# One SBUF arena for all phases, memory rows made token-major inside the chains, and 8-row stationaries

## The chip, the cores and the metric

The kernel runs on one core of one Trainium2 chip. The metric is the device time of one execution in microseconds. Three executions of the kernel before took 4016.91, 4025.89 and 4031.85 us, median 4025.89.

## The reference

A transformer block with a recurrent memory, forward and backward. x is 2048 tokens of 448 values, in bf16. `h = x + A(layernorm(x))`, `h2 = h + B(layernorm(h))`, and the outputs are h2 and the gradients of x, mem0 and the seven weights for a given gradient of h2.

A cuts the tokens into 64 segments of 32. Segment s sees 8 memory tokens in front of its own 32 (40 rows in all); with 16 heads of 256 (4096 columns) it computes

```
h = concat(mem, xs);  q, k, v = h Wq, h Wk, h Wv
p = softmax(mask(q k^T / 16));  o = (p v) Wo
mem = o[:8]            # the next segment's memory
out = o[8:]
```

where the mask hides earlier rows' view of later keys, and memory rows see everything. B is `(silu(x Wg) * (x Wu)) Wd` with 1792 hidden columns. Memory ties the 64 segments into a chain, forward and, for the gradients, back.

## The kernel before

Four phases follow each other in one program; the Tile framework orders each engine's instructions, and what stands under `k.prio.crit()` goes ahead of the rest.

**Start.** SP loads Wq and Wo, POOL loads Wv and Wk (L97 and L98 in `load_rows_padded`, L257). Behind them on SP stand mem0 (L270) and every other tile of x (L280), whose layernorm goes to XN in DRAM.

**forward_chain.** A tile is 128 tokens, four segments; r = 0..3 is a segment's place in it. Per segment PE runs `wpass` for q and k (L378: 128 matmuls each of 40 columns), scores (L406), the 8 memory rows' v (L413), the softmax's transposes (L442), P V (L450), the memory rows' output through Wo (L460) and four small matmuls that turn the 8 rows into the next segment's memory columns (L469, L472). The memory rows of V come through SBUF: `v_sb` is copied into V by DMAs on SP and ACT (L431). As filler PE computes v for a later tile (L359; through `vstg` to Vx in DRAM, read back at L369) and, at r = 3, the tile's output px (L492). L460 takes 32 columns per chunk as stationary (`oTm`, 8 used, 24 zero) and writes strips of 32 rows, one for each j % 4, of a bank from the pool `ps` (6 banks). For the weight gradients the chain leaves in DRAM: Q and K and V per segment, P, the tile's head outputs feature-major (X_o, 1 MB, L499 on SP), and of the 8 memory rows M_o (L481) and MT (L485), each by a POOL copy and a POOL DMA.

**ffn_phase.** Eight groups of two tiles, forward and backward. SP transposes WdT (L112, L114), WgT (L525) and WuT (L526) from DRAM around the first group's loads (L548, L556); its gate, up and hidden values leave token-major by SP transposes into `tstg` and POOL stores (L537, L538). At its end dh goes to DH and, in bf16, to DHb.

**backward_chain.** SP first loads WoT (L112, L114), then WkT, WvT and WqT (L303), all by DMA transposes, then dhx from DHb (L660). Per segment, in reverse: dO = do WoT (L703), its transposed copy dO_sb (L709, a DMA transpose on SP), dP (L715), dS, three head products (L694) and three passes of the memory rows' gradient (L746, again 32-column stationaries, into one bank `pH`) which give the earlier segment's memory gradient (L753, L755). SP loads vT, Q_sb, K_sb by DMA transposes (L681, L683, L685). POOL writes DMT (L765), copies each of k, v, q's memory columns into one buffer `x8` and stores it to M_k, M_v, M_q (L768, L769); at r = 0 px (L774) and the three X stores of 1 MB (L776).

**tail_phase.** Weight gradients: operands in token-major rows are multiplied with other rows, summed over 20 blocks, 16 tiles and 4 blocks of 16 x 8 memory rows. `load_half` brings one half (2048 of 4096 columns) of X_o, X_v, X_k or X_q: 16 DMA transposes on SP (L811), then four times a POOL load of M (L816), two packing copies (L819 DVE, L820 ACT) and a DMA transpose from SBUF (L822), into a ring of 36 buffers. The other operand is DC (from DHb, and DMT) or HC (from XN, and MT), whose memory rows come by POOL loads, copies and PE transposes (L834 to L839). `rows_by_d` (L869) makes dWo and dWdown, `d_by_e` (L853) the others: per block six matmuls of 128 stationary columns and, for the last 64 of 448, two of 64 columns side by side, into seven accumulators. Results go through three buffers `wres` to ACT's DMA queue. In between POOL, DVE and ACT make dx (L902 to L909). Gate, up and down read DGP, DU (L917) and Zt (L934) by plain loads.

## Time and profile before

The profiled execution took 4031.56 us, its span is 4029.7 us.

| engine | busy us | share of the span |
|---|---|---|
| PE | 3318.0 | 82% |
| DVE | 1369.7 | 34% |
| ACT | 809.4 | 20% |
| POOL | 785.7 | 19% |

| stage | from us | to us |
|---|---|---|
| start, until PE's first q pass | 0 | 58.5 |
| forward chain | 58.5 | 1320.3 |
| FFN's loads before its first matmul | 1320.3 | 1357.4 |
| FFN | 1357.4 | 1695.5 |
| until the backward chain's first matmul | 1695.5 | 1775.9 |
| backward chain | 1775.9 | 3066 |
| tail | 3066 | 4029.7 |

A line such as "L853 PE MATMUL acc<-xt,HC" names the source line, the engine, the operation, the tile written and the tiles read; x is a count. SPq is SP's queue, where DMA transposes hold the engine while their descriptors are made. "DMA share" is the busy share of the core's 16 DMA engines; it can read slightly over 1. "PEclk" is the granted clock of PE as a fraction of full speed. In a window's row the first number is its length, then each engine's busy time and count.

### The profile page before, as it was taken

To read this page: it belongs to the slowest core of one execution; us is meant where nothing else is said; L and a number is where in the kernel's file an instruction comes from. 1 tells how busy PE (TensorE), PEld (TensorE's weight loads), DVE (VectorE), ACT (ScalarE), POOL (GpSimd) and SP (SyncE) were. 2 spreads that over 40 slices of the span, in tenths; PEclk is the share of its full clock that TensorE was granted. 3 is DMA by queue.
4 is the path that set the end of the run, shared out by engine and by line. 5 is a ranking of instruction groups with operands and counts; after the bars stand their busy time and mean duration, and the time that the engine had idled before them with its cause. 6 is when DMAs were issued, how large, how long until landed. Compare 5 with 4: busy or idle time off the path is not lost.

```text
span 4029.7 us, 120360 instructions
## 1 busy us (share of the span) xinstructions
PE 3318.0 (82%) x53974; PEld 2056.4 (51%) x53974; DVE 1369.7 (34%) x3032; ACT 809.4 (20%) x1914; POOL 785.7 (19%) x1669
## 2 busy tenths in 40 slices
PE   3888988998988588738898898898996566887999
...
PEclk9999999999998799869899999998997788998999
...
GB/s 236 139 136 147 140 146 140 142 148 142 133 136 115 207 166 192 165 225 158 172 181 154 164 184 149 152 164 167 172 170 161 188 207 171 159 167 159 196 183 48
DMA packets 1201433, 653.00 MB, mean 162 GB/s; under 512 B 1093012, under 2 KB 1127604, under 8 KB 1191316
## 3 DMA queue, kind: packets, MB, share of 16 engines
...
## 4 chain that ended last, share of the span: by engine, by line
PE 62%; DMA 16%; SPq 7%; issue 5%; DVE 4%; ACT 3%; POOL 1%; ACTq 0%; DVEq 0%; POOLq 0%
PE acc L853 11%; PE psf L378 11%; PE psf L746 7%; PE fx L774 6%; PE psf L703 5%; DMA dO_sb<-doT 4%; PE psf L460 4%; SPq L811 3%; PE acc L869 2%; PE psf L694 2%; PE psf L413 2%; PE fx L492 2%; PE fx L359 2%; PE psf L469 1%; DMA out_dram<-wres 1%
## 5 line engine op out<-in xcount | busy, mean ns | idle before, releaser
L853 PE MATMUL acc<-xt,HC 128*128 128x512 bf16 (+1 forms) x1920 | 446.8, 405 | 95.3 <-ACT wres L77 70.4
L853 PEld LDWEIGHTS <-HC 128*128 128x128 bf16 (+1 forms) x1920 | 157.9, 103 | 384.2 <-issue 278.7
L703 PE MATMUL psf<-do_roll,WoT_sb 128*128 128x40 bf16 x8192 | 217.6, 180 | 85.3 <-POOL do_roll L663 80.5
L703 PEld LDWEIGHTS <-WoT_sb 128*128 128x128 bf16 x8192 | 216.4, 96 | 97.2 <-issue 82.8
L869 PE MATMUL acc<-DC,xt 128*128 128x448 bf16 x640 | 147.6, 393 | 114.9 <-ACT wres L77 35.5
L378 PEld LDWEIGHTS <-Wq_sb 128*128 128x128 bf16 x8192 | 231.3, 100 | 19.6 <-issue 8.2
L378 PE MATMUL psf<-hT_roll,Wq_sb 128*128 128x40 bf16 x8192 | 231.6, 184 | 5.7 <-DVE hT_roll L472 5.4
L75 DVE CAST wres<-acc 128x512 bf16<-128x512 f32 (+1 forms) x87 | 56.5, 669 | 496.1 <-PE acc L853 277.1
L378 PE MATMUL psf<-hT_roll,Wk_sb 128*128 128x40 bf16 x8192 | 219.3, 180 | 0.5 <-issue 0.4
L378 PEld LDWEIGHTS <-Wk_sb 128*128 128x128 bf16 x8192 | 213.8, 97 | 0.9 <-issue 0.7
L869 PEld LDWEIGHTS <-xt 128*128 128x128 bf16 x864 | 87.9, 104 | 213.2 <-issue 79.6
L75 DVE CAST doT<-psf 128x480 bf16<-128x480 f32 (+1 forms) x128 | 73.6, 575 | 245.7 <-PE psf L703 245.7
L77 ACT CAST wres<-acc 128x512 bf16<-128x512 f32 (+2 forms) x87 | 47.6, 551 | 539.4 <-PE acc L853 264.3
L359 PE MATMUL fx<-Wv_sb,hx 128*128 128x512 bf16 x512 | 135.4, 386 | 17.2 <-DMA hx<-XN 9.9
L413 PE MATMUL psf<-Wv_sb,memT_pad 128*32 128x512 bf16 x2048 | 147.8, 381 | 0.2
L460 PE MATMUL psf<-Wo_sb,oTm 128*32 128x448 bf16 x2048 | 143.4, 436 | 2.8
L774 PE MATMUL fx<-WqT_sb,blkq 128*128 128x448 bf16 x512 | 130.8, 371 | 0.0
L774 PE MATMUL fx<-WvT_sb,blkv 128*128 128x448 bf16 x512 | 128.2, 369 | 0.0
L746 PE MATMUL psf<-WvT_sb,dvm 128*32 128x448 bf16 x2048 | 123.9, 388 | 3.4 <-DVE dvm L75 0.4
L774 PE MATMUL fx<-WkT_sb,blkk 128*128 128x448 bf16 x512 | 124.6, 354 | 0.0
L492 PE MATMUL fx<-Wo_sb,xblk 128*128 128x448 bf16 x512 | 118.1, 356 | 0.0
L746 PE MATMUL psf<-WqT_sb,dqm 128*32 128x448 bf16 x2048 | 110.7, 357 | 3.5 <-DVE dqm L75 0.4
...
## 6 DMA issues: line engine op xcount, KB each, us to landing
...
KT<-kT_363 SPq DMA_DIRECT2D x32, 512.0 KB
...
VG<-V_365 SPq DMA_DIRECT2D x32, 512.0 KB
...
VG<-V_366 SPq DMA_DIRECT2D x32, 512.0 KB
...
```

The source lines that it names most:

```text
L75: nc.vector.tensor_copy(out=out, in_=in_)
L359: nc.tensor.matmul(pv[:, 0:512], lhsT=hx[t][:, kc, :], rhs=Wv_sb[:, kc, n * 512:(n + 1) * 512], start=(kc == 0), stop=(kc == KC - 1))
L378: nc.tensor.matmul(pss[b][:, jj * L:(jj + 1) * L], lhsT=W_sb[:, kc, c * P:(c + 1) * P], rhs=hT_roll[:, kc, sl, :], start=(kc == 0), stop=( ...
L413: nc.tensor.matmul(pV[b][32 * j:32 * j + 32, 0:512], lhsT=memT_pad[:, kc, :], rhs=Wv_sb[:, kc, n * 512:(n + 1) * 512], start=(kc == 0), st ...
L460: nc.tensor.matmul(pO[32 * (j % 4):32 * (j % 4) + 32, 0:D], lhsT=oTm[:, j, :], rhs=Wo_sb[:, cj(j), :], start=(j < 4), stop=(j >= MC - 4), ...
L492: nc.tensor.matmul(px[:, 0:D], lhsT=xblk[:, j, :], rhs=Wo_sb[:, cj(j), :], start=(j == 0), stop=(j == MC - 1))
L703: nc.tensor.matmul(pss[b][:, jj * L:(jj + 1) * L], lhsT=WoT_sb[:, kc, c * P:(c + 1) * P], rhs=do_roll[:, kc, sl, :], start=(kc == 0), stop ...
L746: nc.tensor.matmul(pH[32 * (j % 4):32 * (j % 4) + 32, 0:D], lhsT=dm_pad[nm][:, j, :], rhs=WT[:, cj(j), :], start=(wi == 0 and j < 4), stop ...
L774: nc.tensor.matmul(px[:, 0:D], lhsT=blk[nm][:, j, :], rhs=WT[:, cj(j), :], start=(wi == 0 and j == 0), stop=(wi == 2 and j == MC - 1))
L811: nc.sync.dma_start_transpose(out=x_t[:].rearrange("p (j n) -> p j n", n=P), in_=dr["X_" + nm][t][:, hf * 2048:(hf + 1) * 2048])
L853: nc.tensor.matmul(o, lhsT=lhs, rhs=rhs_of(b, g), start=(b == 0), stop=(b == nblk - 1), skip_group_check=True)
L869: nc.tensor.matmul(pa[i][:, 0:D], lhsT=lhs_of(b, i), rhs=rhs_of(b), start=(b == 0), stop=(b == nblk - 1))
```

## The change

Two kinds of thing change: where data lives, and how the memory rows reach the tail.

All phases share three SBUF areas, W (124 KB per partition), A (65 KB) and B (8.25 KB), each one tile; every buffer is a fixed range of one, and a phase's buffers lie over those of the phase before, so that an instruction waits for the last readers of its range and not for a pool to close. PSUM is one pool of 5 `ps` banks, 2 `fx` and 1 `po`. In the order rows the areas are called arW, arA and arB; the line numbers tell what is meant.

In the forward chain a finished tile of head outputs is transposed to token-major by two DMA transposes on SP through the two staging buffers of v_proj and stored by POOL (`to_token_major`, L390, L392); the memory rows of 16 segments are gathered in `mblk` and `mh` and go the same way, as blocks 16 to 19 of X_o and XN (L504). In the backward chain the memory rows' do are gathered in `dmr` and become blocks 16 to 19 of DHb (L783). M_k, M_v, M_q are stored straight from the stationaries; M_o, MT, DMT and the copies into `x8` are gone. The tail loads X_o plainly (L843), X_v, X_k and X_q by DMA transposes as before (L845), and the memory blocks of v, k, q by a POOL load, two packing copies and 16 PE transposes with two copies out of PSUM (L859). `d_by_e` runs the full matmuls of four blocks (L875) before their half-width ones (L880). The ring has 33 buffers, results have 8. The memory stationaries of L460 and L746 have 8 columns; the 24 rows of each strip that they no longer write are zeroed once, in a bank of their own. At the start x and mem0 stand first on SP and ACT, and POOL loads all weights in the order Wq, Wk, Wv, Wo.

```diff
+class _Arena:
+
+
+    def __init__(self, pool, name, kb):
+        self.n = int(kb * 512)
+        self.t = pool.tile([P, self.n], BF16, name=name)
...
-            m0f = work.tile([P, DP], BF16, name="m0", tag="xtmp", bufs=2)
-            m0 = m0f[0:M, :]
-            nc.sync.dma_start(out=m0[:, 0:D], in_=MEM0)
...
-            for t in range(NT):
-                x_tf = work.tile([P, DP], BF16, name="x_t0", tag="xtmp", bufs=2)
-                (nc.sync if t % 2 == 0 else nc.gpsimd).dma_start(out=x_tf[:, 0:D], in_=X2[t * P:(t + 1) * P, :])
...
-        k.load_rows_padded(Wv_sb, Wv2, nc.gpsimd)
-        k.load_rows_padded(Wq_sb, Wq2, nc.sync)
-        k.load_rows_padded(Wk_sb, Wk2, nc.gpsimd)
-        nc.sync.dma_start(out=Wo_sb[:], in_=Wo2.rearrange("(c p) d -> p c d", p=P))
...
+    pO = k.po1()
+    nc.vector.memset(pO[:], 0.0)
...
+    nc.sync.dma_start(out=v_sb[0:M, 0:D], in_=MEM0)
...
+    def stats(t):
+        q = nc.sync if t % 2 == 0 else nc.scalar
+        x_t = xblk_b[0].rearrange("p a b -> p (a b)")[:, (t % 4) * DP:(t % 4) * DP + D]
+        q.dma_start(out=x_t, in_=X2[t * P:(t + 1) * P, :])
...
+    for t in range(2):
+        stats(t)
+    pad_rows(k, Wq_sb, k.Wq2, nc.gpsimd)
+    pad_rows(k, Wk_sb, k.Wk2, nc.gpsimd)
+    pad_rows(k, Wv_sb, k.Wv2, nc.gpsimd)
+    nc.gpsimd.dma_start(out=Wo_sb, in_=k.Wo2.rearrange("(c p) d -> p c d", p=P))
...
+    for t in range(2, NT):
+        stats(t)
...
+    def to_token_major(blk, t):
+        for hf in range(2):
+            ot = stg()
+            nc.sync.dma_start_transpose(out=ot.rearrange("p (a b) -> p a b", b=P),
+                                        in_=blk[:, 16 * hf:16 * hf + 16, :].rearrange("p c n -> p (c n)"))
+            nc.gpsimd.dma_start(out=dr["X_o"][t][:, hf * 2048:(hf + 1) * 2048], in_=ot)
...
-                k.evac(oTm[:, 12 * b:12 * b + n, 0:M], v[:, :, SEG:L], "vsv"[b])
-            pO = k.ps1()
+                k.evac(o8[:, 12 * b:12 * b + n, :], v[:, :, SEG:L], "vsv"[b])
             for j in range(MC):
-                nc.tensor.matmul(pO[32 * (j % 4):32 * (j % 4) + 32, 0:D], lhsT=oTm[:, j, :], rhs=Wo_sb[:, cj(j), :],
+                nc.tensor.matmul(pO[32 * (j % 4):32 * (j % 4) + M, 0:D], lhsT=o8[:, j, :], rhs=Wo_sb[:, cj(j), :],
...
-        o8 = work.tile([P, 32, M], BF16, name="o8", bufs=2)
-        nc.gpsimd.tensor_copy(out=o8[:], in_=oTm[:, :, 0:M])
-        nc.gpsimd.dma_start(out=dr["M_o"][s], in_=o8[:].rearrange("p c m -> p (c m)"))
-        m8 = work.tile([P, KC, M], BF16, name="m8", bufs=2)
-        nc.gpsimd.tensor_copy(out=m8[:], in_=hT_roll[:, :, sl, SEG:L])
-        nc.gpsimd.dma_start(out=dr["MT"][s], in_=m8[:].rearrange("p c m -> p (c m)"))
...
+        nc.gpsimd.tensor_copy(out=mh[:, :, jm * M:(jm + 1) * M], in_=hT_roll[:, :, sl, SEG:L])
+        nc.gpsimd.tensor_copy(out=mblk[:, :, jm * M:(jm + 1) * M], in_=o8)
...
-            nc.sync.dma_start(out=dr["X_o"][t], in_=xblk[:].rearrange("p c n -> p (c n)"))
...
+            to_token_major(xblk, t)
+        if jm == 15:
+            to_token_major(mblk, NT + s // 16)
+            mrow = stg()
+            nc.sync.dma_start_transpose(out=mrow[:, 0:DP].rearrange("p (a b) -> p a b", b=P),
+                                        in_=mh.rearrange("p c n -> p (c n)"))
+            r0 = (NT + s // 16) * P
+            nc.gpsimd.dma_start(out=dr["XN"][r0:r0 + P, :], in_=mrow[:, 0:DP])
...
+    transposed_rows(k, WoT_sb, k.Wo2, woT_tmp)
...
+    prep_tile(NT - 1)
+    load_seg(NSEG - 1)
+    for (Wsrc, WT) in ((k.Wk2, WkT_sb), (k.Wv2, WvT_sb), (k.Wq2, WqT_sb)):
+        nc.sync.dma_start_transpose(out=WT, in_=Wsrc)
...
-                    nc.tensor.matmul(pH[32 * (j % 4):32 * (j % 4) + 32, 0:D], lhsT=dm_pad[nm][:, j, :], rhs=WT[:, cj(j), :],
+                    nc.tensor.matmul(pH[32 * (j % 4):32 * (j % 4) + M, 0:D], lhsT=d8[nm][:, j, :], rhs=WT[:, cj(j), :],
...
-        d8 = work.tile([P, KC, M], BF16, name="d8", bufs=2)
-        nc.gpsimd.tensor_copy(out=d8[:], in_=do_roll[:, :, sl, SEG:L])
-        nc.gpsimd.dma_start(out=dr["DMT"][s], in_=d8[:].rearrange("p c m -> p (c m)"))
...
+        nc.gpsimd.tensor_copy(out=dmr[:, :, jm, :], in_=do_roll[:, :, sl, SEG:L])
+        if jm == 0:
+            nc.sync.dma_start_transpose(out=dhx, in_=dmr.rearrange("p c s m -> p (c s m)"))
+            r0 = (NT + s // 16) * P
+            nc.gpsimd.dma_start(out=dr["DHb"][r0:r0 + P, :], in_=dhx.rearrange("p c n -> p (c n)"))
         for nm in "kvq":
-            x8 = work.tile([P, 32, M], BF16, name="x8", bufs=1)
-            nc.gpsimd.tensor_copy(out=x8[:], in_=dm_pad[nm][:, :, 0:M])
-            nc.gpsimd.dma_start(out=dr["M_" + nm][s], in_=x8[:].rearrange("p c m -> p (c m)"))
+            nc.gpsimd.dma_start(out=dr["M_" + nm][s], in_=d8[nm].rearrange("p c m -> p (c m)"))
...
+    def load_x(nm, hf):
+        tiles = []
+        for t in range(NT if nm != "o" else NB):
+            x_t = ring()
+            src = dr["X_" + nm][t][:, hf * 2048:(hf + 1) * 2048]
+            if nm == "o":
+                nc.sync.dma_start(out=x_t, in_=src)
+            else:
+                nc.sync.dma_start_transpose(out=x_t.rearrange("p (j n) -> p j n", n=P), in_=src)
+            tiles.append(x_t)
+        return tiles
+
+    def load_m(nm, hf, tiles):
+        for g in range(NG):
+            nc.gpsimd.dma_start(out=ld, in_=dr["M_" + nm][g * 16:(g + 1) * 16].rearrange(
+                "s p (c m) -> p s c m", m=M)[:, :, hf * 16:(hf + 1) * 16, :])
+            nc.vector.tensor_copy(out=pk[:, 0:8], in_=ld[:, :, 0:8, :].rearrange("p s c m -> p c s m"))
+            nc.scalar.copy(out=pk[:, 8:16], in_=ld[:, :, 8:16, :].rearrange("p s c m -> p c s m"))
+            x_t = ring()
+            for q in range(2):
+                pt = k.ph1()
+                for i in range(8):
+                    nc.tensor.transpose(pt[:, i * P:(i + 1) * P], pk[:, 8 * q + i].rearrange("p s m -> p (s m)"), ident[:, :])
+                k.evac(x_t[:, q * 1024:(q + 1) * 1024], pt[:, 0:1024])
+            tiles.append(x_t)
+
+    nc.gpsimd.dma_start(out=DCt, in_=dr["DHb"].rearrange("(t p) d -> p t d", p=P)[:, :, 0:D])
+    xo = load_x("o", 0)
...
+        pa = accs(7)
+        for b0 in range(0, nblk, 4):
+            for b in range(b0, min(nblk, b0 + 4)):
+                for kc in range(KC - 1):
                     for g in range(2):
                         w = widths[g]
...
+                        nc.tensor.matmul(pa[2 * kc + g][:, 0:w], lhsT=lhs_of(b)[:, kc * P:(kc + 1) * P], rhs=rhs_of(b, g),
+                                         start=(b == 0), stop=(b == nblk - 1), skip_group_check=True)
+            for b in range(b0, min(nblk, b0 + 4)):
+                for g in range(2):
+                    w = widths[g]
+                    nc.tensor.matmul(pa[6][64 * g:64 * g + 64, 0:w], lhsT=lhs_of(b)[:, (KC - 1) * P:D], rhs=rhs_of(b, g),
+                                     start=(b == 0), stop=(b == nblk - 1), skip_group_check=True)
```

SP in the forward chain, where a tile has just been finished. L369 and L371 load V's rows, L431 and L438 copy the memory rows' v into V, L477/L482 and L479/L484 store K and V. Before:

```order
L479 DMA VG<-V_366 128x2048
L499 DMA X_o<-xblk 128x4096
L369 DMA V_366<-Vx 32x2048 x2
L477 DMA KT<-kT_363 128x2048
L431 DMA V_365<-v_sb 8x1024 x2
```

The same place in the change:

```order
L484 DMA VG<-arA 128x2048
L390 DMA_TRANSPOSE arA<-arA 128x16x128 x2
L371 DMA arA<-Vx 32x2048 x2
L482 DMA KT<-arA 128x2048
L438 DMA arA<-arA 8x1024 x2
```

Where one store of X_o stood, two transposes from SBUF to SBUF stand, ahead of the next loads of V, K's store and the v copy.

SP from the last FFN group into the backward chain. L537 and L553 transpose FFN results, L112/L240 WoT, L303/L694 WkT, WvT and WqT, L660/L668 is dhx. Before:

```order
L537 DMA_TRANSPOSE tstg<-g 128x14x128
L112 DMA_TRANSPOSE WoT_sb<-in_A_Wo_dram 128x4096 x3
L114 DMA_TRANSPOSE woT_tmp<-in_A_Wo_dram 128x4096
L303 DMA_TRANSPOSE WkT_sb<-in_A_Wk_dram 128x32x448
L115 DMA WoT_sb<-woT_tmp 64x4096
L303 DMA_TRANSPOSE WvT_sb<-in_A_Wv_dram 128x32x448
L303 DMA_TRANSPOSE WqT_sb<-in_A_Wq_dram 128x32x448
L660 DMA_TRANSPOSE dhx<-DHb 128x4x128
L681 DMA_TRANSPOSE vT<-VG 128x16x128
```

In the change, from the last two FFN transposes on (L674 and L675 are vT and Q_sb, L676 K_sb, L729 dO_sb; the three of WoT, L240, stand three rows further ahead, between other L553):

```order
L676 DMA_TRANSPOSE arW<-KT 128x16x128
L553 DMA_TRANSPOSE arA<-arW 128x14x128
L553 DMA_TRANSPOSE arW<-arA 128x14x128
L694 DMA_TRANSPOSE arW<-in_A_Wq_dram 128x32x448
L241 DMA_TRANSPOSE arA<-in_A_Wo_dram 128x4096
L668 DMA_TRANSPOSE arA<-DHb 128x4x128
L674 DMA_TRANSPOSE arA<-VG 128x16x128
L242 DMA arW<-arA 64x4096
L675 DMA_TRANSPOSE arW<-QT 128x16x128
L694 DMA_TRANSPOSE arW<-in_A_Wk_dram 128x32x448
L729 DMA_TRANSPOSE arA<-arA 128x16x128
L694 DMA_TRANSPOSE arW<-in_A_Wv_dram 128x32x448
```

WoT moved up between the FFN's own transposes, WqT ahead of dhx, and WkT and WvT behind it, on both sides of the first segment's dO_sb.

SP in the tail, its last rows. Before, each half is 16 transposes from DRAM and 4 from SBUF:

```order
L811 DMA_TRANSPOSE xt<-X_o 128x16x128 x16
L822 DMA_TRANSPOSE xt<-mpk 128x16x128 x4
L811 DMA_TRANSPOSE xt<-X_o 128x16x128 x16
L822 DMA_TRANSPOSE xt<-mpk 128x16x128 x4
L811 DMA_TRANSPOSE xt<-X_v 128x16x128 x16
```

In the change:

```order
L843 DMA arW<-X_o 128x2048 x21
L843 DMA arA<-X_o 128x2048 x3
L843 DMA arW<-X_o 128x2048 x3
L843 DMA arA<-X_o 128x2048 x3
L843 DMA arW<-X_o 128x2048
L845 DMA_TRANSPOSE arW<-X_v 128x16x128 x18
L845 DMA_TRANSPOSE arA<-X_v 128x16x128 x4
```

The transposes of X_o and all transposes from SBUF are gone from SP; X_o comes by plain loads.

796 lines of the change are left out of this document (376 added, 420 removed).

## The prediction

> **What bounds the kernel now.** I read the page's 40 slices first (PE's busy tenths and its granted clock), then cut the span into its stages with the table of windows, and after that asked in each stage what the idle engine waited for.
>
> ```profile
> span 4029.7 us, 120360 instructions
> PE   3888988998988588738898898898996566887999
> PEclk9999999999998799869899999998997788998999
> ```
>
> ```profile
> core 0: us, PE busy (x) PEld busy (x) DVE busy (x) ACT busy (x) POOL busy (x), PEclk, DMA share, GB/s
> 0.00:58.50 58.50, 2.39 (x10) 0.94 (x11) 7.31 (x22) 2.13 (x5) 23.12 (x36) 1.00 0.83 270
> 58.50:99.50 41.00, 31.52 (x461) 18.23 (x460) 26.08 (x73) 14.36 (x33) 16.52 (x47) 0.92 0.58 184
> 121.10:1320.30 1199.20, 1071.80 (x25224) 773.39 (x25223) 485.70 (x1089) 309.89 (x735) 213.92 (x479) 0.93 0.39 139
> 1320.30:1357.40 37.10, 0.00 (x0) 0.00 (x1) 2.33 (x6) 2.15 (x3) 11.06 (x21) 0.55 1.04 221
> 1695.50:1775.90 80.40, 0.00 (x1) 0.11 (x2) 5.13 (x12) 0.56 (x1) 12.72 (x22) 0.52 1.08 240
> 1775.90:3066.00 1290.10, 1161.16 (x22522) 755.23 (x22521) 483.19 (x1216) 271.34 (x783) 366.44 (x824) 0.94 0.82 164
> 3066.00:3290.00 224.00, 111.93 (x486) 50.01 (x486) 63.47 (x159) 25.49 (x39) 49.68 (x69) 0.74 1.05 196
> 3290.00:3798.60 508.60, 411.95 (x1782) 150.58 (x1781) 36.99 (x65) 48.57 (x66) 26.46 (x23) 0.89 0.90 167
> ```
>
> PE is busy 90% of both chains (1071.8 of 1199.2 us, 1161.2 of 1290.1), so there little is to be had from anything but PE's own instructions. It does next to nothing for 58.5 us at the start, 37.1 before the FFN and 80.4 before the backward chain. In the first 224 us of the tail PE works half the time at a granted clock of 0.74, while the DMA engines are past full share (1.05); in the next 508.6 it works 81%. So the idle time sits at the joints and in the tail, and there transfers end last.
>
> **The tail.** Its stages by PE's own work, and who moves the operands:
>
> ```profile
> L853 PE MATMUL acc<-xt,HC x1920: 376/379/636, 3333.7 to 3875.4; 128*128 128x512 bf16 x144, 128*64 128x512 bf16 x48
> L853 PE MATMUL acc<-xt,HNa x512: 272/379/403, 3875.7 to 3979.6; 128*128 128x512 bf16 x94, 128*128 128x256 bf16 x34, 128*64 128x512 bf16 x33, 128*64 128x256 bf16 x10
> L869 PE MATMUL acc<-GOa,xt 128*128 128x448 bf16 x224 | 42.5, 352 | 0.0
> L811 SPq DMA_TRANSPOSE xt<-X_v x32: 2016/3046/11175, 3266.4 to 3410.3; - x32
> L811 SPq DMA_TRANSPOSE xt<-X_q x32: 2048/3133/9222, 3618.0 to 3762.0; - x32
> L822 SPq DMA_TRANSPOSE xt<-mpk x32: 1718/2002/8284, 3138.7 to 3795.9; - x32
> ```
>
> From 3066 the tail takes 4029.7 - 3066 = 963.7 us: 267.7 until the first L853 at 3333.7 (the output projection's gradient, "o"), 541.7 for v, k and q, 104 for gate and up, 43 for down (42.5 in the third row), about 7 to land the last result. The transposes of v start at 3266.4 and those of q at 3618.0: 351.7 us for four halves, 88 each. That is SP's rhythm, not PE's: 2 passes x 20 blocks x 1.74 us are 70.
>
> *The o stage.* The 32 X_o transposes and the four steps that gather DMT and MT through a staging tile go; 40 plain 512 KB loads stay, and DCt in one load. In the fourth row below 16 plain loads of 448 KB were issued in 19.7 us, as many as SP's waits let by, so 20 of 512 KB are some 28. PE's own work is 640 matmuls (2 halves x 16 chunks x 20 blocks) at the third row's 42.5/224 = 0.190 us, 121.6. The first loads need only slots that the last WoT pass or the last px has left. I add 12 us for DCt's load (row below: 10.0) and the joints between result groups: 134 in place of 267.7.
>
> ```profile
> DC<-DHb POOLq DMA_DIRECT2D x1, 1792.0 KB, 10.0
> L816 POOL DMA_DIRECT2D mld<-M_v x8: 1148/1156/1166, 3264.6 to 3432.0; - x8
> DMA to landing us min/median/max: 6.9/7.6/16.2
> L917 SPq DMA_DIRECT2D xt<-DGP x16: 319/343/974, 3798.6 to 3818.0; - x16
> L820 ACT COPY mpk<-mld x32: 1044/1045/1047, 3089.3 to 3794.8; 128x1024 bf16<-128x1024 bf16 x32
> PE acc L853 <- ACT wres L77: 75.0, 24, 14.7
> DVE wres L75 <- DMA out_dram<-wres: 151.7, 36, 14.1
> 3644.06:3645.80 1.74, 1.74 (x10) 1.00 1.21 280
> ```
>
> *v, k, q.* A block is six full matmuls and a side-by-side pair of half-width ones; the last row is one block with PE at full clock: 1.74 us. Seven slots of 512 columns at 0.190 x 512/448 = 0.217 are 1.52, so each trip full-half-full costs 0.22. One trip for four blocks leaves 1.52 + 0.055 = 1.575. Twelve passes of 20 blocks: 378 in place of 418. Added to PE are 6 x 64 transposes of 128x128; from below each costs 128/512 of 0.217 = 0.054, from above a whole 0.217: 21 to 83 us; they stream 128 columns, so I take 30. Moved off the DMA engines are four 512 KB transposes per half. At share 0.90 the DMA engines were busy 0.90 x 508.6/6 = 76 us per half; without four of twenty transposes that is at best 61, at worst still 76, and I take 64. So PE, 63 + 5 = 68, ends last, unless its order makes it wait: each memory block needs a load (7.6), a copy (1.045) and its transposes in turn, with one load buffer. The first two are fetched ahead, the other two are not, some 3 us each, so 6 x 6 = 36. Sum 378 + 30 + 36 = 444 in place of 541.7; from 378 + 21 = 399 to 6 x (76 + 8) = 504, where the transfers still set the pace and the load chain adds 8 a half. Eight result buffers for three take the waits of the sixth and seventh rows (results that wait for a store, PE that waits for them): inside the 444, since they hide in SP's rhythm today. Gate and up: 64 blocks x 0.165 = 11 off 104, so 93.
>
> Tail: 134 + 444 + 93 + 43 + 7 = 721, which is **-243** (bounds -170 to -290).
>
> **The joints.** Three places, in one table of rows:
>
> ```profile
> L270 SPq DMA_DIRECT2D m_143<-in_A_mem_dram x1: 37804/37804/37804, 2.5 to 2.5; - x1
> GB/s 98 411 426 431 308 243 320 270 417 413 249 306 339 323 40 0 93 174 114 156 169 233 90 43 246 67 194 249 293 313 283 83 45 321 23 193 187 258 32 166
> 1341.45 6.55 SPq L525
> 1356.76 11.33 SPq L526
> 1710.26 1.98 DMA DHb<-dh_b
> 1724.97 4.08 SPq L114
> 1729.09 12.96 SPq L303
> 1742.74 16.81 SPq L303
> 1759.58 13.12 SPq L303
> 1772.81 2.62 DMA dhx<-DHb
> ```
>
> Start: on SP the load of mem0 stood 37.8 us behind Wq and Wo, the x tiles behind it, and the second segment began only at 99.5. Now x and mem0 go first on SP and ACT, and the four weights follow each other on POOL. 14.7 MB at 300 to 430 GB/s (second row, 40 slices of the first 130 us) need 34 to 49 us whatever the queue; Wv is third, so the v rows start near 40 and segment 0 ends near 75: **-25** (0 to -40). The Trainium skill, "DMA: Bandwidth & Descriptors", section "Issuing engines are not separate DMA queues", says that DMAs of all issuing engines run on the same 16 engines, so another queue saves issue time alone; taken strictly the x rows would crawl beside the weights and this term would be about 0, and the sum 3766. The row of L270 shows the other case, an issue that is blocked, and that one the move does cure.
>
> Before the FFN: the same weight transposes (WdT with its rest from 1320.3 to 1341.5, then 6.6 and 11.3 us) now begin when the last k pass has left its slots, 17 us sooner, but one stands ahead of the last segment's v copy, and WuT ahead of the first hnT: **-4** (+10 to -15).
>
> Before the backward chain: from DHb's landing at 1712.2 SP ran WoT (12.7 us, to 1725.0) and then 4.1 + 13.0 + 16.8 + 13.1 us of weights before dhx. Now WoT and WqT are ahead of it; WkT (13) and WvT (16.8) follow Q_sb, with segment 63's dO_sb transpose between. About 50 come off the gap and some 25 come back as that segment's wait: **-25** (0 to -45).
>
> **The chains.** Forward: 40 SBUF-to-SBUF transposes are added to SP's order (two after each fourth segment's VG store, four more where a group of 16 ends), with their POOL stores; one 1 MB SP store per tile and 128 POOL stores go.
>
> ```profile
> 1306.59 0.65 SPq L431
> PE psf L450 <- DMA V_366<-v_sb: 26.7, 13, 2.3
> L709 SPq DMA_TRANSPOSE dO_sb<-doT x64: 1664/2187/9418, 1783.8 to 3026.5; - x64
> PE psf L694 <- DMA dO_sb<-doT: 65.0, 20, 8.0
> ```
>
> SP's next urgent item is the v copy V<-v_sb, late in the following segment (the last one, first row, 14 us before the chain's end at 1320.3, px of 6 us included, in segments of 1199.2/62 = 19.3 us); two transposes at 2 to 3 us of SP (L822 and L811 above) are over by then, at a DMA share of 0.39. I charge 0.6 us for each of 20 groups: **+12** (0 to +160, if 8 us land on the chain each time). The 8-column stationaries stream the same 448 columns into the same strips: 0. Five ps banks and one fixed in place of six: the fixed one was held through the same part, 0. Backward: 192 POOL copies and 64 stores go; no PE wait of that stage names them, but X, M and the dO_sb transpose (third and fourth rows) share the DMA engines: **-6** (+15 to -25). FFN groups: same chain, 0.
>
> **Sum.** -243 - 25 - 4 - 25 + 12 - 6 = -291 on the profiled execution's 4031.6 us (span 4029.7 and 1.9 around it): 3741. The median of the runs shown is 4025.9, 5.7 lower, so 3735; I say **3738**.
>
> **The rivals.** *B, the tail stays with its transfers:* halves of 84, as in the upper bound: 504 for 444, so about 3800. For it: share 1.21 in a block at full PE speed. Against it: the SBUF-source transposes ran one at a time, each behind its copies. Chance 0.22. The Trainium skill, "TensorE: Matmul & The Clock Gate", Part 1, says that PE falls to half clock after an idle window of about 3.4 us; the windows agree (0.74 where PE works half the time), and by it 24 stalls in B would each cost about half a window more, 41 us, and B would end nearer 3840.
>
> *C, the forward chain pays for the transposes:* they meet the v copy or the two staging buffers that v_proj shares, 8 us at 20 places: 3738 - 12 + 160 = 3886. For it: PV waits for V<-v_sb already (second row of that fence). Chance 0.12.
>
> *E, the grouping does nothing:* full and half matmuls cost their switch anyhow: 240 x 0.165 + 11 = 51, so 3789. Against it is 1.74 against 1.52. Chance 0.06.
>
> *D, slower:* PE is in order, and the memory blocks' transposes stand inside the first pass of each half. If every one of the 24 waits for its whole chain, a load as slow as the slowest, 16.2 us, plus 1.15 of issue, 1.05 and 2, that is 24 x 20.4 = 490, less the 36 charged: 4192. From 291/24 + 1.5 = 13.6 us for each block on it is slower than before. Against it: two blocks of each half are fetched ahead. Chance 0.05.
>
> **How the numbers follow.** Forecast 0.55 (its own range 3675 to 3815, the terms' bounds added as squares since they need not come together), B 0.22, E 0.06, C 0.12, D 0.05. The range 3655 to 3880 holds the forecast, B, E and about half of C, some 0.85. Less than 0.5%, 20 us, can't be told from no change here. A, B, C and E are all faster; D is slower; for stalls that add up without one name I give D's side a little more: faster 0.92, same 0.02, slower 0.06.
>
> **What would show it.** Right: first L875 about 140 us after the last px, v, k, q halves of 70 to 78 us, a block of four at 6.3 us with one change of width; a second forward segment near 75; a first L703 near 1725 of the old time. Wrong: idle PE before L859 with a POOL load behind it (D); L845 on SP without a gap and PE idle (B); forward r = 0 segments above 21 us with L438 late (C). The forecast as a whole falls if the two chains, two thirds of the span, run more than 1 us a segment differently.

## The result and the profile after

The changed kernel took 3904.01 us, median of four executions (3883.62 to 3926.88); the kernel before took 4021.40 beside it, median of four (3999.45 to 4031.85). The ratio is 0.9717, 95% interval 0.9638 to 0.9795: faster by about 117 us. The prediction was 3738 with a range from 3655 to 3880: the sign was right, and well over half of the expected gain did not come. The profiled execution after took 3888.53 us, its span is 3886.4, against 4029.7 before: 143.3 less, some 26 more than the medians differ.

Two lines of the page of after, and its table of windows, cut by PE's own work as before (forward chain from the first to the last hand-over of memory, up to the first FFN matmul, from the last FFN matmul to the first WoT matmul, backward chain, then the tail's output projection, its v, k and q, and the rest):

```profile
PE   3888898899888668864898898899999967888899
...
PEclk9999999999998789986998999999999988999999
```

```profile
90.20:1315.70 1225.50, 1078.57 (x25235) 765.44 (x25233) 489.33 (x1095) 313.12 (x740) 169.90 (x399) 0.93 0.47 151
1315.70:1387.00 71.30, 21.65 (x417) 14.31 (x415) 9.53 (x22) 7.06 (x13) 15.24 (x27) 0.66 1.05 241
1726.30:1765.10 38.80, 0.43 (x3) 0.10 (x1) 3.32 (x8) 0.56 (x1) 10.27 (x17) 0.56 1.14 228
1765.10:3082.00 1316.90, 1167.24 (x22523) 743.29 (x22523) 476.30 (x1216) 274.10 (x783) 260.37 (x578) 0.94 0.86 176
3082.00:3250.00 168.00, 129.17 (x641) 64.53 (x640) 57.63 (x144) 8.50 (x17) 28.03 (x50) 0.89 0.78 216
3250.90:3741.10 490.20, 422.79 (x2296) 185.84 (x2295) 55.40 (x94) 74.08 (x94) 26.46 (x23) 0.93 0.75 160
3741.10:3886.40 145.30, 134.86 (x736) 65.27 (x736) 14.68 (x24) 12.06 (x25) 0.00 (x0) 0.98 0.33 113
```

The tail is still where PE is idle without cause of its own: 39 of 168 us in the output projection, 67 of 490 in v, k and q, at a DMA share of 0.75 to 0.78. That speaks against the transfers ending last there, and the runs below decide it. The sum of the prediction, beside what the two traces give for each term (joints are counted between PE's own instructions, and the edges agree to 0.4 us):

| term | predicted us | measured us |
|---|---|---|
| start, up to the first hand-over (98.65 → 90.2) | −25 | −8.4 |
| forward chain, first to last hand-over (1196.7 → 1225.5) | +12 | +28.8 |
| last hand-over to the first FFN matmul (62.1 → 71.3) | −4 | +9.2 |
| FFN (338.1 → 339.3) | 0 | +1.2 |
| gap before the backward chain (80.4 → 38.8) and that chain (1290.2 → 1316.9) | −31 | −14.9 |
| tail: output projection (267.7 → 168.8) | −134 | −98.9 |
| tail: v, k, q (541.7 → 490.2) | −98 | −51.5 |
| tail: rest (154.2 → 145.7) | −11 | −8.5 |
| sum | −291 | −143 |

What PE waits for in the tail of after (the view of waits, PE from 3082 us on; total, times, longest):

```profile
PE psf L896 <- DVE arA L75: 38.8, 5, 20.0
PE fx L875 <- ACT arA L77: 24.8, 7, 6.6
PE ph L859 <- DVE arA L853: 19.2, 11, 3.0
PE psf L875 <- ACT arA L77: 9.7, 1, 9.7
```

L75 and L77 are the copies of results out of PSUM on DVE and on ACT. PE waits for accumulators to be emptied, by two engines that in these stages are busy 5 to 34% of the time (8.5 and 57.6 of 168 us, 74.1 and 55.4 of 490). One of DVE's waits (3082 to 3200 us) and ACT's order of instructions in two places of the timeline say what they do instead:

```profile
DVE lnb_m_61567 L249 <- DMA dxn_ld<-DXN: 9.7, 1, 9.7
```

```profile
3166.59 13.06 ACTq L910 DMA_DIRECT2D out_dram<-arA  x4
3179.69 0.53 ACT L77 CAST arA<-psf 128x448 bf16<-128x448 f32 x1 [12.70 <-DVE arA L75]
...
3503.34 9.42 ACTq L922 DMA_DIRECT2D out_dram<-arA  x5
3512.81 0.59 ACT L77 CAST arA<-fx 128x512 bf16<-128x512 f32 x1 [8.95 <-DMA arW<-X_q]
```

DVE stands in ln_bwd of dx (L249), which waits for one single-buffered load after another. On ACT the rows of 13.06 and 9.42 us are spans, with pauses in them. All stores of v, k and q as they were issued, and then the same two places in narrower windows:

```profile
L922 ACTq DMA_DIRECT2D out_dram<-arA x96: 333/410/914, 3306.0 to 3752.4; - x96
...
3166.59 0.82 ACTq L910 DMA_DIRECT2D out_dram<-arA  x2
...
3178.78 0.87 ACTq L910 DMA_DIRECT2D out_dram<-arA  x2
...
3503.34 2.42 ACTq L922 DMA_DIRECT2D out_dram<-arA  x4
```

One issue takes ACT 0.41 us at the median. In the first place the third store waits 11.3 us for a copy that DVE makes behind ln_bwd (that copy ends at 3178.75). In the second the fifth store waits 6.6 us, until a transposing load of X_q, issued by SP at 3505.56, has landed at 3512.35: store and load use the same completion semaphore, and the row behind it names that load. By the semaphore updates of the trace 18 stores waited for such landings in v, k and q, 57 us in all. The next copies of results stand behind those stores, each engine working in order.

### The profile page after: what moved, and what is told of

Read it like the earlier page. It is cut to its first block, busy times and chain, and to the rows that moved or that the text cites. A ratio compares the mean times of both kernels' runs of the same rounds, so it can differ in the third digit from the quotient of the medians.

```text
span 3886.4 us, 120434 instructions
## 1 busy us (share of the span) xinstructions
PE 3278.9 (84%) x54326; PEld 2060.7 (53%) x54326; DVE 1366.1 (35%) x3034; ACT 811.9 (21%) x1893; POOL 597.4 (15%) x1253
## 4 chain that ended last, share of the span: by engine, by line
PE 64%; DMA 19%; issue 5%; DVE 4%; SPq 4%; ACT 3%; POOL 1%; ACTq 0%; DVEq 0%; POOLq 0%
PE psf L381 11%; DMA arA<-arA 10%; PE po L765 8%; PE psf L875 7%; PE psf L724 5%; PE fx L792 5%; PE po L465 4%; PE psf L703 3%; PE psf L562 2%; PE psf L422 2%; PE fx L494 2%; PE fx L362 2%; PE fx L880 2%; ACT arA L77 2%; PE psf L474 1%
## 5 line engine op out<-in xcount | busy, mean ns | idle before, releaser
L75 DVE CAST arA<-psf 128x480 bf16<-128x480 f32 (+4 forms) x709 | 403.1, 575 | 936.7 <-PE psf L381 323.5
L77 ACT CAST arA<-psf 128x384 bf16<-128x384 f32 (+4 forms) x883 | 404.8, 489 | 1325.5 <-PE psf L381 343.4
L381 PEld LDWEIGHTS <-arW 128*128 128x128 bf16 x16384 | 437.4, 98 | 32.4 <-issue 20.6
L381 PE MATMUL psf<-arA,arW 128*128 128x40 bf16 x16384 | 439.4, 182 | 17.2 <-issue 11.6
L792 PE MATMUL fx<-arW,arA 128*128 128x448 bf16 x1536 | 370.6, 366 | 13.8 <-issue 13.8
L75 DVE CAST arB<-psf 128x96 bf16<-128x96 f32 (+2 forms) x640 | 179.4, 287 | 525.7 <-PE psf L703 284.7
L765 PE MATMUL po<-arW,arB 128*8 128x448 bf16 x6144 | 345.2, 368 | 19.9 <-DMA arW<-in_A_Wv_dram 11.1
L77 ACT CAST arB<-psf 128x96 bf16<-128x96 f32 (+1 forms) x384 | 115.2, 300 | 735.7 <-PE psf L703 566.7
L875 PE MATMUL psf<-arW,arA 128*128 128x512 bf16 x990 | 260.1, 391 | 9.7 <-ACT arA L77 9.7
L724 PE MATMUL psf<-arA,arW 128*128 128x40 bf16 x8192 | 220.4, 180 | 49.7 <-POOL arA L671 38.4
L724 PEld LDWEIGHTS <-arW 128*128 128x128 bf16 x8192 | 219.1, 96 | 69.7 <-issue 55.5
L875 PEld LDWEIGHTS <-arA 128*128 128x128 bf16 x1440 | 138.5, 101 | 212.3 <-issue 73.9
L562 PE MATMUL psf<-arA,arW 128*128 128x256 bf16 x1344 | 167.3, 287 | 79.2 <-DMA arA<-arA 39.1
L792 PEld LDWEIGHTS <-arA 128*128 128x128 bf16 x1536 | 143.5, 106 | 135.6 <-issue 53.0
L562 PEld LDWEIGHTS <-arW 128*128 128x128 bf16 x1344 | 138.1, 103 | 110.6 <-issue 84.7
L465 PE MATMUL po<-arW,arB 128*8 128x448 bf16 x2048 | 146.2, 441 | 2.9 <-DVE arB L75 0.3
L896 PE MATMUL psf<-arW 128*128 128x448 bf16 x450 | 98.8, 371 | 38.8 <-DVE arA L75 38.8
L456 PE MATMUL psf<-arB,arA 128*128 128x80 bf16 x1024 | 53.4, 211 | 90.3 <-DMA arA<-arA 74.6
```

Of the source, the lines that this page charges most:

```text
L75: nc.vector.tensor_copy(out=out, in_=in_)
L77: nc.scalar.copy(out=out, in_=in_)
L381: nc.tensor.matmul(pss[b][:, jj * L:(jj + 1) * L], lhsT=W_sb[:, kc, c * P:(c + 1) * P], rhs=hT_roll[:, kc, sl, :], start=(kc == 0), stop=( ...
L465: nc.tensor.matmul(pO[32 * (j % 4):32 * (j % 4) + M, 0:D], lhsT=o8[:, j, :], rhs=Wo_sb[:, cj(j), :], start=(j < 4), stop=(j >= MC - 4), sk ...
L562: nc.tensor.matmul(ps[:, f2 * 256:(f2 + 1) * 256], lhsT=Wt[:, kc, c * P:(c + 1) * P], rhs=xT[:, kc, :], start=(kc == 0), stop=(kc == KC - 1))
L724: nc.tensor.matmul(pss[b][:, jj * L:(jj + 1) * L], lhsT=WoT_sb[:, kc, c * P:(c + 1) * P], rhs=do_roll[:, kc, sl, :], start=(kc == 0), stop ...
```

## The experiments

Each edit is made on the changed kernel, and each ratio is to the kernel before, run on the same chip; after itself stands at 0.9717 [0.9638, 0.9795]. The backward chain, which no edit touches, came out between 1301 and 1348 us in these profiles, the forward chain, where no edit touches it, between 1222 and 1246, and the output projection with dx in its old place between 169 and 181. So a stage is read by its own length, and a total only with its interval.

### Tail: dx moved behind the weight gradients

```diff
-            for t in range(NT):
-                rows = slice(t * P, (t + 1) * P)
-                dh_t = k.f32("f2", D, "dh_ld")
...
+    for t in range(NT):
+        rows = slice(t * P, (t + 1) * P)
+        dh_t = A(33.5 + 2 * (t % 2), 2 * D).bitcast(FP32)
...
+        dxn = A(37.5 + 2 * (t % 2), 2 * D).bitcast(FP32)
...
```

(the lines taken out stand ahead of the copies of the output projection's results in DVE's order, the new ones behind the q blocks, with two buffers for each load in place of one)

> Compared with the changed kernel (span 3886.4 us; its o stage, first L896 to first L875, 168.6 us). The 16 tiles of the layernorm gradient, whose instructions stand between the o stage's result copies in VectorE's order, are moved behind the last memory block of q, with two buffers for each of their loads. Theory A (the o results wait behind VectorE's wait for these loads): the 20 us gap after the first result group goes and the o stage takes 130 to 145 us; the total falls by 25 to 40 us unless the moved work stalls the gate and up passes, which have 95 us in all. Rival (the o stage is paced by its loads and by the X_v transposes on the DMA engines): the o stage stays within 5 us of 168.

Measured: 3842.24 us, ratio 0.9518 [0.945, 0.9587]. The output projection took 122.3 us in place of 168.8, v, k and q 490.8 as before, and the last stage 160.1 in place of 145.7, since DVE's dx stands there now. In a window from the end of the backward chain into the output projection PE does not pause at all:

```profile
3060.00:3180.00 120.00, 119.97 (x633) 61.74 (x632) 8.33 (x15) 8.01 (x15) 4.21 (x4) 1.00 0.87 248
```

So the 46.5 us were DVE's queue. With it gone the stage is PE's own 640 x 0.190 = 121.6 us; the 12 us that the prediction had added for DCt and the joints were not needed.

### Tail: result stores issued by GpSimd

```diff
-                nc.scalar.dma_start(out=oo[c * P:(c + 1) * P, :], in_=r)
+                nc.gpsimd.dma_start(out=oo[c * P:(c + 1) * P, :], in_=r)
...
-                    nc.scalar.dma_start(out=o2[kc * P:min(D, (kc + 1) * P), e0:e0 + 512], in_=r)
+                    nc.gpsimd.dma_start(out=o2[kc * P:min(D, (kc + 1) * P), e0:e0 + 512], in_=r)
```

> The result stores of o, v, k and q are issued by GpSimd in place of ScalarE; nothing else moves. Theory B (the first pass of each half takes 50 to 56 us and not 38 because ScalarE, which copies results and memory blocks, sits for up to 13 us on issuing five stores while SyncE's transposes fill the DMA rings): the five first passes after the first fall from 50-52 us to 42 to 46, some 30 to 45 us in all, and the second passes stay at 31.0. Rival C (they wait for the loads of the memory blocks, one buffer each): first passes stay at 49 to 52 us.

Measured: 3868.07 us, ratio 0.9582 [0.9455, 0.971]; v, k and q 455.2 in place of 490.2, the output projection 170.5. The waits of PE in its tail:

```profile
PE psf L896 <- DVE arA L75: 42.3, 3, 20.3
PE ph L859 <- DVE arA L853: 41.4, 11, 11.7
```

All waits for ACT are gone but for 0.7 us, since the stores that wait for landings no longer stand ahead of ACT's copies. The run does not tell the store's place in ACT's order from the shared semaphore; no run gave the stores of ACT semaphores of their own. What the waits had covered shows now: the chain of a memory block (load, packing copy, transposes) takes 41.4 us of PE where it took 19.2.

### Tail: both

> Both of the two edits before. If theory A and theory B hold and the two do not share their time: the tail from the first L896 to the end, 804 us in the changed kernel, falls by the sum of the two, to 725 to 750; the total to about 3810 to 3835 us. If both edits cure one and the same wait, the tail falls by the larger of the two alone.

Measured: 3819.54 us, ratio 0.9462 [0.9395, 0.9529]; output projection 122.4, v, k and q 470.6, the rest 158.2. The two gains do not add up fully: the memory blocks' chain grows once more (first row), and in the last stage, where dx stands now, one copy of a result keeps PE 15.5 us (second row, at 3681.7 us):

```profile
PE ph L859 <- DVE arA L853: 51.0, 11, 10.5
PE psf L875 <- DVE arA L75: 15.5, 1, 15.5
```

### Tail: two buffers for the memory rows, four for dx's loads

```diff
-    ld = A(33.5, 16, 16, M)
-    pk = A(37.5, 16, 16, M)
+    ld_b = [A(33.5, 16, 16, M), B(4, 16, 16, M)]
+    pk_b = [A(37.5, 16, 16, M), A(29.5, 16, 16, M)]
...
+            ld, pk = ld_b[g % 2], pk_b[g % 2]
```

(with the two edits above, dx's loads rotating over four places, and a ring of 32 in place of 33)

> Result stores on GpSimd and the layernorm gradient moved behind q as in the third run, now with four buffers for its loads, and two load and two pack buffers for the memory blocks (one ring slot less). In the third run PE still waits 51 us for the memory blocks' chain of load, copy and transposes. If that is the rest of theory C, the first passes of v, k, q fall from 41-53 us to 38 to 40, the three gradients take 415 to 425 us in place of 470.6, and gate, up and down return from 158 to about 146; total 3755 to 3775. If the transfers themselves set the pace, v, k, q stay above 450.

Measured: 3784.81 us, ratio 0.939 [0.926, 0.952]; output projection 122.4, v, k and q 428.2, the rest 141.0. What PE still waits for longest in its whole tail (lines past 849 are one further down):

```profile
PE ph L860 <- DVE arW L75: 13.0, 4, 5.8
PE ph L860 <- DVE arA L75: 4.4, 1, 4.4
```

The tail is 122.4 + 428.2 + 141.0 = 691.6 us, under the 721 of the prediction: its transfers, its slots and PE's own work do allow the time that was predicted, and what stood in the way were the queues of DVE and ACT and one pair of buffers. The granted clock over v, k and q is 0.98 here, where it was 0.93 in after.

### Tail: full and half-width matmuls not grouped

```diff
-        for b0 in range(0, nblk, 4):
-            for b in range(b0, min(nblk, b0 + 4)):
+        for b0 in range(0, nblk, 1):
+            for b in range(b0, min(nblk, b0 + 1)):
```

> The changed kernel with full and half-width matmuls switched at every block again, as before the change. If a switch there and back costs 0.22 us (1.74 against 1.52 a block), a second pass of 20 blocks takes 34.8 us in place of 31.0, and the 16 passes of v, k, q, gate and up together up to 45 us more where PE is the limit: the total rises by 30 to 50 us. If the grouping does nothing (rival E), the second passes stay at 31.0.

Measured: 3948.64 us, ratio 0.9796 [0.9658, 0.9935]. A second pass over a half, where nothing waits, in after and then in this kernel:

```profile
3391.20:3422.60 31.40, 31.40 (x164) 13.21 (x163) 2.57 (x4) 2.24 (x4) 0.00 (x0) 1.00 0.91 163
```

```profile
3428.70:3463.00 34.30, 34.30 (x163) 12.37 (x162) 2.48 (x5) 2.24 (x4) 0.00 (x0) 1.00 0.97 174
```

From the first full matmul to the last half-width one it is 31.0 us against 34.0 for 20 blocks, at full granted clock in both. 15 of 20 trips full-half-full are saved, so a trip costs 0.20 us; the prediction had 0.22, and 31.5 per pass. v, k and q took 514.8 us in place of 490.2, gate, up and down 9.5 more; the total cannot be told from after's by its interval.

### Forward: without the transposes

```diff
-            nc.sync.dma_start_transpose(out=ot.rearrange("p (a b) -> p a b", b=P), in_=...)
-            nc.gpsimd.dma_start(out=dr["X_o"][t][:, hf * 2048:(hf + 1) * 2048], in_=ot)
+            nc.gpsimd.dma_start(out=dr["X_o"][t][:, hf * 2048:(hf + 1) * 2048], in_=...)
```

> The forward chain's 36 transposes of head outputs to token-major are left out: the tile and the gathered memory rows are stored as they are by two GpSimd stores (dWo is then computed from feature-major data and is not the reference's; the work of all later stages is the same). Theory D (the 2.2 us by which segments with r = 0 are longer than before, 20.5 for 18.3, come from these transposes): r = 0 segments return to 18.3 to 18.8 and the forward chain is 25 to 33 us shorter. Rival (they come from the moved stores, or from five PSUM banks in place of six): r = 0 segments stay at 20 us or more.

The four transposes of `mh` stay, so 36 of the 40 are left out, and dWo is summed from rows in the wrong order. Measured: 3922.03 us, ratio 0.9716 [0.9657, 0.9776]. The forward chain fell from 1225.5 to 1210.7 us. By place in the tile, an r = 0 segment took 18.3 us before, 20.5 after and 19.1 here (20.1 to 21.2 in the other profiles); r = 1 to 3 took 18.7, 19.5 and 20.7 before and 18.6, 19.4 and 20.7 after. So the transposes cost about 1.4 of the 2.2 us that a first segment lost on the mean. The loss is not even: the three segments behind a gathered block of 16 took 23.5 to 24.3 us in after, the twelve others 18.5 to 21.2. Of the 0.8 us a segment that remain here, most sits in two of those three (21.6 and 23.0 us); no run shows the cause. The total did not fall, since what follows the chain became longer: 94.5 us to the first FFN matmul in place of 71.3. The rows of SP there (L240 WdT, L437 the v copy, L581 and L582 WgT and WuT):

```profile
1316.91 15.76 SPq L240 DMA_TRANSPOSE arW<-in_B_w_down_dram  x1
...
1332.77 1.34 SPq L437 DMA_DIRECT2D arA<-arA  x2
...
1338.40 31.06 SPq L581 DMA_TRANSPOSE arW<-in_B_w_gate_dram  x1
...
1370.83 18.94 SPq L582 DMA_TRANSPOSE arW<-in_B_w_up_dram  x1
```

The last segment's v copy stands 15.8 us behind a weight transpose, and the first hn behind 31 and 19 us of them.

### Before the FFN: the last v copy on ACT

```diff
-                eng = nc.sync if j % 2 == 0 else nc.scalar
+                eng = nc.sync if j % 2 == 0 and s < NSEG - 1 else nc.scalar
```

> Only in the last segment the four copies of the memory rows' v go out on ScalarE's queue alone. In the changed kernel that segment's copy stands on SyncE behind a 7 us transpose of WdT and lands 17 us after its data were ready. If that is what makes the stretch from the last hand-over to the first FFN matmul 71.3 us and not 62, it falls to 58 to 63; if the weight transposes are the limit (they all have to run before the first FFN matmul), it stays above 68.

Measured: 3911.44 us, ratio 0.9704 [0.957, 0.9839]; the stretch is 69.9 us, so the expected 58 to 63 failed. The copies are issued from 1335.3 to 1344.0 us without SP, and PE still waits:

```profile
1346.85 0.71 PE L456 MATMUL psf<-arB,arA 128*128 128x80 bf16 x8 [10.39 <-DMA arA<-arA]
```

SP's order ahead of the copy alone is not the cause: behind the copy WgT and WuT still stand ahead of hn, and the same DMA engines carry them.

### Before the FFN: weight transposes held back

```diff
         if gi == 0:
+            for tl in (WdT_sb[:, 0, 0:1], WdT_sb[:, 1, 0:1], WdT_sb[:, 2, 0:1], wdT_tmp[:, 0:1],
+                       WgT_sb[:, 0, 0:1], WuT_sb[:, 0, 0:1]):
+                nc.vector.tensor_copy(out=tl, in_=hnT[:, 0, G * P - 1:G * P])
             transposed_rows(k, WdT_sb, Wd2, wdT_tmp)
```

> The changed kernel with the transposes of the FFN's weights (WdT, WgT, WuT) held back: one column of each destination is written first with a copy of the first group's transposed hn, so the transposes can start only when hnT is there. Nothing is left out. Theory G (the last forward segment's v copies and the hn transposes stand behind 16 to 23 us of weight transposes on the shared DMA engines): the stretch from the last hand-over to the first FFN matmul falls from 71.3 to 48 to 58 us; the FFN's first group may then wait up to 15 us for WdT, since gate and up of one group give it about 20 us of cover, so the total gains 5 to 20 us. Rival (the stretch is its own chain of attention, output product, statistics and transposes, whose length the weights don't set): 66 to 72 us, and the FFN is longer by the wait for WdT, so that the total is the same or worse by 10 us.

Measured: the stretch is 46.2 us in place of 71.3, the FFN 344.2 in place of 339.3: 20 us from the two. The wait ahead of the FFN's first matmul, in after and then here (PE, from the last segment on):

```profile
PE psf L562 <- DMA arA<-arA: 33.0, 1, 33.0
```

```profile
PE psf L562 <- DMA arA<-arA: 17.6, 1, 17.6
```

Theory G holds for its stretch. The total is 3904.84 us, ratio 0.9648 [0.9606, 0.969]: 0.7% below after's, as 20 us or a little more would have it, but the intervals overlap, so the total neither shows the gain nor denies it. In this profile the backward chain took 1347.7 us in place of 1316.9, the output projection 174.8 in place of 168.8, and this edit touches neither.

### Start: x ahead of everything

Two kernels load all x tiles first into arena units that Wo takes later, and the weights in the order Wv, Wq, Wk. In the first one the statistics of tiles 4 to 15 stand behind Wo's load into the same units, so they read Wo in place of x, and what is computed from them is not the reference's; DVE no longer waits there for x but for Wo, so it is no clean test of theory F. Its first hand-over came at 82.7 us, where theory F had 55 to 65, after 23.25 MB; its total was 3916.53, ratio 0.9717 [0.9561, 0.9873].

> At the start all 16 tiles of x are loaded at once into buffers of their own, and the weights follow in the order Wv, Wq, Wk, Wo, gated by the first four tiles' XN stores. Theory F (the small x and XN transfers crawl behind 14.7 MB of weights on the shared DMA engines, 14 to 27 us each, and VectorE waits for them in front of the copies that v_proj needs): the first memory hand-over, at 90.2 us in the changed kernel, comes at 55 to 65 us, a gain of 25 to 35. Rival (the 39 us of weights and the first two tiles' v projections are the floor): it stays above 80.

The second has them ahead of it:

```diff
+    x_l = [W(96 + 0.875 * t, D) for t in range(NT)]
+    for t in range(NT):
+        (nc.sync if t % 2 == 0 else nc.scalar).dma_start(out=x_l[t], in_=X2[t * P:(t + 1) * P, :])
...
     v_proj(1, 0, 8)
+    for t in range(4, NT):
+        stats(t)
+    nc.gpsimd.dma_start(out=Wo_sb, in_=k.Wo2.rearrange("(c p) d -> p c d", p=P))
```

> The changed kernel with its startup in another order: all sixteen x tiles are loaded ahead of everything else into arena units that Wo takes later, their normalised rows go to other units there, the weights are loaded in the order Wv, Wq, Wk, and the statistics of tiles 4 to 15 and the load of Wo stand behind the first two v projections. Nothing is left out. Theory F (the startup lost its gain because small x loads and XN stores stand among 14.7 MB of weight loads on the same 16 DMA engines, and DVE waits for them in order, ahead of the v projections' copies): the first hand-over comes at 68 to 80 us instead of 90.2, and the total falls by 10 to 22 us. Rival (the bytes themselves are the limit, in whatever order: the XN stores and their transposes still stand behind weights): 85 to 92 us, total unchanged.

Measured: 3905.63 us, ratio 0.965 [0.9503, 0.9798], first hand-over at 95.6 us in place of 90.2. Waits of DVE for x fall from 40.8 to 0.8 us, and PE waits as long as ever for the first transposed rows. In after, and then here:

```profile
PE fx L362 <- DMA arA<-XN: 39.4, 1, 39.4
...
DVE stats L82 <- DMA arA<-in_A_x_dram: 40.8, 7, 28.8
```

```profile
PE fx L360 <- DMA arA<-XN: 43.2, 1, 43.2
...
DVE stats L82 <- DMA arW<-in_A_x_dram: 0.8, 1, 0.8
```

The DMA engines are at full share at first, and nearly idle afterwards (two windows of the second kernel):

```profile
20.00:40.00 20.00, 0.00 (x0) 0.00 (x0) 12.24 (x47) 3.21 (x12) 1.78 (x1) 1.00 1.03 342
...
44.00:54.00 10.00, 7.04 (x24) 2.76 (x25) 1.95 (x3) 1.17 (x2) 1.57 (x5) 1.00 0.08 16
```

Theory F falls as a forecast: taking the x loads out of DVE's way does not by itself bring the first hand-over forward. Its rival, that the bytes are the limit, does not follow either, since at 44 to 54 us hardly any move.

### All of it together, without and with a start ordered by data

The first is the tail with two buffers and the late weight transposes. The second adds a start in which Wq and Wk are loaded only when the second tile's transpose is there:

```diff
+    for tl in (Wq_sb, Wk_sb):
+        nc.vector.tensor_copy(out=tl[:, 0, 0:1], in_=hx_b[1][:, 0, 0:1])
+        nc.vector.tensor_copy(out=tl[0:64, 3, 0:1], in_=hx_b[1][0:64, 0, 0:1])
+    pad_rows(k, Wq_sb, k.Wq2, nc.gpsimd)
+    pad_rows(k, Wk_sb, k.Wk2, nc.gpsimd)
```

> e7_two_buffers (tail's result stores on GpSimd, ln_bwd behind the q blocks with four load buffers, two buffers for the memory rows) together with e10's late weight transposes. Nothing is left out. e7 measured 3784.8 us, and e10 took 25.1 us from the stretch ahead of the FFN and gave 4.9 back inside it. If that gain is a gain of the path: 3755 to 3775 us. Rival (what is taken from that stretch comes back later, as e10's total of 3904.8 beside 3904.0 for the changed kernel would have it: its backward chain was 31 us longer): 3780 to 3800 us with a backward chain of 1330 us or more.

Measured: 3780.24 us (3770.16 to 3796.18), ratio 0.9365 [0.9306, 0.9425], with 46.3 us ahead of the FFN, 344.3 in it and a backward chain of 1331.0. The median lies in the rival's range, but the ratio is below the 0.939 of the kernel with two buffers, and by their intervals the two kernels cannot be told apart; whether the backward chain answers to this edit stays open, since it varies as much without it.

> e11_queues_and_late_transposes with the startup ordered by data: four x tiles, then Wv alone, then the transposes of the first two tiles; Wq and Wk are loaded only when the second tile's transpose is there (a copy into one of their columns holds them), the other x tiles and Wo after that. Nothing is left out. e9, which only put the x loads first, had its first transposes wait 43.2 us behind all the weights. Theory F' (weights issued early are what the XN stores and transposes stand behind, so holding Wq and Wk back frees them): first hand-over at 70 to 82 us instead of 90 to 96, total 8 to 20 us under e11's. Rival (the bytes needed before the first hand-over, 11 MB of weights and 4 MB of x and XN at about 285 to 340 GB/s, take the time in any order, and holding some back adds idle time): 88 to 100 us, total the same as e11 or up to 10 us above.

Measured: 3767.47 us (3761.21 to 3807.52), ratio 0.9355 [0.9269, 0.9442]; first hand-over at 93.1 us. That lies in the rival's range of 88 to 100. PE begins earlier (11.8 us of work between 20 and 40 us) and pays for it afterwards; two pieces of the chain of waits in the start:

```profile
41.13 16.54 DMA arW<-in_A_Wk_dram
...
69.96 17.42 DMA arW<-in_A_Wo_dram
```

The first hand-over needs all four weights. Up to it 23.24 MB had moved in before, 23.01 in after and 25.26 here. What lands last is another transfer each time (x in after, XN with x ahead, Wk and Wo here), and the time stays within 6 us of after's. The rival's reason, that the bytes take this time in any order, is not shown by that: the DMA engines were full for a part of the start only, and the kernel that took 82.7 us had moved as many bytes. Two windows of after:

```profile
10.00:50.00 40.00, 3.60 (x8) 1.19 (x9) 5.97 (x15) 1.07 (x4) 14.50 (x14) 1.00 1.03 353
50.00:90.20 40.20, 27.60 (x447) 16.21 (x447) 20.11 (x55) 12.96 (x27) 6.34 (x17) 1.00 0.60 200
```

What holds the start at 90 us stays open.

Both kernels of this section and those with dx moved (alone, with the stores, and with two buffers) are faster than the changed kernel and the one before: their intervals end at or below 0.9587, where after's begins at 0.9638.

## Why the prediction was wrong, and where it was right

- **Tail, output projection.** The step that failed is "12 us for DCt's load and the joints". PE's 121.6 and the removal of the transposes were right (122.3 us with dx out of the way); the joints cost 46.5 us, because ln_bwd of dx stood in DVE's order ahead of the result copies. The step counted loads and PE, and did not ask what DVE was to do next to its copies.
- **Tail, v, k, q.** The step that failed is "eight result buffers for three take the waits of the sixth and seventh rows ... inside the 444". The buffers were enough, but the stores are issued by ACT, which also empties the accumulators, and there wait for copies of DVE and for landings of SP's loads: 35 us by the run with stores on GpSimd. The chain of the memory blocks took 19 us in after and 41 to 51 once ACT was free, for the 36 taken. The 30 us for the blocks' 384 transposes were not too little: eight of them take 0.45 us at full clock, so 0.056 each and 22 in all. What no term of the sum held is the lower clock behind each pause: 0.93 over the 490 us, so some 34 us of clock were not granted. The grouping was right to half a us a pass. Eight transposes and five matmuls at full clock, then matmuls behind a pause of 6.56 us, which start 0.43 us apart in place of 0.22:

```profile
3504.53 0.62 PE L859 MATMUL ph<-ident,arA 128*128 128x128 bf16 x8
3504.98 1.24 PE L875 MATMUL psf<-arW,arA 128*128 128x512 bf16 x5
...
3513.82 1.91 PE L875 MATMUL psf<-arW,arA 128*128 128x512 bf16 x4
3515.53 0.63 PE L875 MATMUL fx<-arW,arA 128*128 128x512 bf16 x1
```

A first pass over a half, with its memory blocks; the second pass behind it stands under "not grouped", at a clock of 1.00:

```profile
3339.00:3391.20 52.20, 39.09 (x222) 17.36 (x220) 6.64 (x12) 10.37 (x12) 4.60 (x4) 0.90 0.69 139
```

- **Rivals of the tail.** B (transfers set the pace) did not happen, though its 504 us for v, k and q lie near the measured 490: DMA share was 0.75, and the same loads fit into 428 in the run with two buffers. E (grouping does nothing) did not happen: 31.0 against 34.0 us. D had the right place, PE in order behind a memory block, but its longest wait was 3.0 us, not 20. The tail's bound from above, 504, held.
- **Start.** The failed step is "segment 0 ends near 75". What stands ahead of it held: the weights, issued from 7.1 us on, had all landed at 55.8, so in 49 us (34 to 49 were said), and the first v matmul came at 42.9, "near 40". Then PE stood 12.0 us for DVE's copies of v, because the statistics of x stood ahead of them in DVE's order and waited 28.8 us for one tile. That wait is shown, and 16.6 us are missing; but the run without it had its first hand-over no earlier, so what else holds the start stays open. The issue that was blocked for 37.8 us is indeed gone. The Trainium skill, "DMA: Bandwidth & Descriptors", section "Issuing engines are not separate DMA queues", had it that DMAs from every issuing engine share the same 16 engines, so that a move to another queue saves issue time alone. This case's trace agrees: one tile of x, 112 KB, took 2.39 us to land ahead of the weights and 27.24 beside them, and the term was −8.4 where the rule, taken strictly, gave about 0 and the sum gave −25.

The two loads of x in the chain of waits, the landing of Wo (issued at 21.55), and PE's wait, in after:

```profile
1.21 2.39 DMA arA<-in_A_x_dram
...
27.74 27.24 DMA arA<-in_A_x_dram
...
arW<-in_A_Wo_dram POOLq DMA_DIRECT2D x1, 3584.0 KB, 34.2
...
PE fx L362 <- DVE arA L75: 13.4, 3, 12.0
```

- **Forward chain.** +28.8 for +12, with the sign and the place right: only r = 0 segments grew, by 2.2 us. The step "0.6 us for each of 20 groups" was too small: about 1.4 for each tile by the run without transposes, and another 0.8 whose cause is open. After's 1225.5 is at the low end of 1222 to 1246 in the other profiles, so the true size may be larger than 28.8. What waits is P V, for the v copy behind them, as the step said: 74.6 us in the whole program, 14.8 of them in the last segment, where before it was 26.7 and 16.0 for V's two buffers: some 17 us more in the chain. DMA share in the chain rises from 0.39 to 0.47. Rival C, 8 us a place, did not happen: 2.2 on the mean, 6.0 at most behind a gathered block. P V's wait for V's other buffer before, and then PE's group of P V in after:

```profile
PE psf L450 <- DMA V_365<-v_sb: 16.0, 10, 2.3
```

```profile
L456 PE MATMUL psf<-arB,arA 128*128 128x80 bf16 x1024 | 53.4, 211 | 90.3 <-DMA arA<-arA 74.6
```

- **Before the FFN.** −4 was predicted, with +10 as its bound, and +9.2 came. Named right as a possibility (one WdT transpose ahead of the v copy, WuT ahead of hnT), priced too low: 25 us by the run that holds the transposes back.
- **Before the backward chain.** The gap fell by 41.6 us where "about 50" was said, and the chain's first segment took the other way 27 where "some 25" was: within the bounds of the term. The "−6" in the rest of that chain came out at −7 up to its last hand-over and +7 behind it, about 0 together, which by the scatter of that chain shows nothing. No run tests the joint.
- **8-column stationaries: 0.** It fits: r = 1 to 3 segments moved by 0.1 us at most. No run tests the edit alone.
- **The forecast's own range.** Its terms' bounds added as squares, without C's, give 3679 to 3823 where 3675 to 3815 was said; nothing hangs on it.

In sum, of the 148 us that are missing, 81 are in the output projection and in v, k and q, and the run with two buffers gets them back and more. About 17 are in the start, 17 in the forward chain, 13 before the FFN, 16 around the backward chain, and 4 in the FFN and the tail's rest. The range failed because every term missed on the same side. The two largest were sums of an engine's own work, and did not ask what else stood in the order of the engines that empty the accumulators; none of the terms held what a pause costs in clock afterwards.
